# Priorities taken from two backward passes of a kernel's own schedule, and G computed in one step instead of two halves

## The chip, the cores and the metric

The kernel runs on one core of one Trainium2 chip. The metric is device time in microseconds of one execution, the median of three runs. Lower is better.

## The reference

Attention over a packed set of 32 queries, attention of all tokens over that packed result, and then two dense layers with different non-linearities.

```python
# q, k, v: [8, 8, 576, 64], p: [8, 8, 32, 64], all float32
def sm_attn(qq, kk, vv):
    s = scale * np.matmul(qq, kk.transpose(0, 1, 3, 2))
    s = s - np.max(s, axis=-1, keepdims=True)
    a = np.exp(s)
    a = a / (np.sum(a, axis=-1, keepdims=True) + 1e-09)
    return np.matmul(a, vv)
p_packed = sm_attn(p, k, v)
out = sm_attn(q, p_packed, p_packed)
x = out.transpose(0, 2, 1, 3).reshape(4608, 512)
# first dense layer: w_in 512x1024, w_out 1024x512
h = x @ w_in
solu = h * softmax(h)
ln = (solu - mean(solu)) / np.sqrt(var(solu) + 1e-06) * g_ln
x = ln @ w_out
# second dense layer: w_in 512x2048, w_out 2048x512
r = np.maximum(x @ w_in2, 0.0)
return (r * r) @ w_out2
```

The dense weights arrive as 64-bit floats and are decoded to float32 on the chip.

## The kernel before

**Three stages.** Attention and the first dense layer come first; then the first product of the second layer ("z"), then its last product ("o"). All large products split each operand into a rounded part and a remainder (`hi_op`, `lo_op`) and add three products (`mm`, lines 404 to 406). In z and o each 2x2 block product is done with seven products in place of eight, with sums and differences of blocks made on VectorE.

**Stage one** goes over 16 units, a batch entry and a group of four heads each. `pack` loads k and q, turns them (`kT`, `qT`), forms scores `s` with the packed queries (line 560 in the first four units, line 478 later), reduces their maximum `mx` and its negative `nmx` on VectorE, takes the exponential on ScalarE, transposes it (`pt`, line 588), multiplies by v (`ppp`), scales it (`pp`) and transposes that (`ptp`, `ppq`). `unpack` forms the scores of all tokens with `ppq`, normalises them (`a`, `aT`), and multiplies `ppq` by `w_in` into G, 1024 columns in two halves of 512, each in one bank of PSUM (`pg`, line 648). Each half is copied out by ScalarE and then its remainder by VectorE. So attention and `w_in` are folded: `h_tile` gets h of 128 tokens as `aT` times G (`ph`), normalises it and transposes it (`ptv`); `y_stage` multiplies 256 tokens by `w_out` (`py`) and writes to DRAM. For h, the remainders `al` of `aT` are made on VectorE.

**Strips.** z works on six strips of 768 tokens, eight groups of seven products each, and writes its result to DRAM (`g_dram`). o reads it back as `ga`, six strips again, seven products over eight chunks each; `cb` is the split operand. The tiles of `ga` lie in the slots that `y` held in z.

**The planner.** Nothing above runs in program order. Each piece of work is an `Op` with a duration estimate for its engine, an urgency, and its dependencies. `Plan.order` simulates PE, ScalarE, VectorE, GpSimd and one serial DMA server forward in time: of the operations that are ready for a free engine, the one with the lowest urgency goes first. The order in which they start there is the order in which `emit` writes them out, and so the order of the instructions on each engine's queue and of the DMAs on SyncE's queue. Urgencies are written by hand: a formula of the unit or tile number with offsets that stand as constants at the top (`QA`, `GA`, `T0`, `DT`, `WD`, `CS` and so on). A load of n bytes is planned as n/358 ns on the server and lands 2200 ns later:

```python
plan.op(DMA, max(430.0, nbytes / 358.0), at, lambda: queue.dma_start(out=out_(), in_=in_()), r=r, w=w, lag=2200 + spare)
```

**Banks.** Four banks of PSUM (`bank`, a shared ring) serve `s`, `pt`, `ppp`, `ptp`, `pg`, `ptv`, `py` and, later, `pw`, `pz`, `pa`. An operation that needs a bank waits in the plan until `claim` finds one free. `ph` and `px` have banks of their own.

Of the kernel before, what the change touches and what calls it, by code (L numbers as in the profile page):

```python
# [19 lines left out]
PE, ACT, DVE, POOL, DMA = range(5)  # L20
# [70 lines left out]
class Plan:  # L91

    WINDOW = 3413.0

    @staticmethod
# [21 lines left out]
    def either(self, engines, urgency, fn, r=(), w=(), lag=0, claim=(), port=False):  # L120
# [24 lines left out]
        deps.discard(i)  # L145
        self.ops.append(Op(engines, urgency, fn, lag, bufs, deps, port))

    def order(self):
        ops = self.ops
        users = [[] for _ in ops]  # L150
        left = [len(o.deps) for o in ops]
        able = [[] for _ in range(5)]
        busy = [False] * 5
        events = []
        uses = {}
        pe_busy, pe_warm = {}, [False]
        port = 0.0

        def pe_end(t, ns):

            while ns > 1e-6:
                w = int(t / self.WINDOW + 1e-9)
                while len(pe_warm) <= w:
                    share = pe_busy.get(len(pe_warm) - 1, 0.0) / self.WINDOW
                    pe_warm.append(share > 0.74 or (share > 0.5 and pe_warm[-1]))
                slow = 1 if pe_warm[w] else 2
                d = min(ns * slow, (w + 1) * self.WINDOW - t)
                pe_busy[w] = pe_busy.get(w, 0.0) + d
                t += d
                ns -= d / slow  # L170
            return t

        for i, o in enumerate(ops):
            for d in o.deps:
                users[d].append(i)
            for b in o.bufs:
                uses[b] = uses.get(b, 0) + 1
            if not o.deps:
                heapq.heappush(events, (0.0, i, "ready"))
        order = []  # L180

        def claim(i):
            need = [b for b in ops[i].bufs if b.ring and b.ring.shared and b.slot is None]
            for n, b in enumerate(need):
                if len(b.ring.free) <= sum(c.ring is b.ring for c in need[:n]):
                    b.ring.queue.append((ops[i].urgency, i))
                    return False
            for b in need:
                b.slot = b.ring.free.pop(0)
            return True  # L190

        def take(e, t):
            nonlocal port
            while not busy[e] and able[e]:
                _, i = heapq.heappop(able[e])
                o = ops[i]
                if o.engine is not None:
                    continue
                o.engine = e
                busy[e] = True  # L200
                order.append(i)
                if e == POOL or e == DVE and o.port:
                    port = self.span = max(t, port) + o.engines[e]
                else:
                    self.span = pe_end(t, o.engines[e]) if e == PE else t + o.engines[e]
                heapq.heappush(events, (self.span, i, "free"))
                heapq.heappush(events, (self.span + o.lag, i, "done"))

        while events:
            now = events[0][0]  # L210
            while events and events[0][0] <= now:
                t, i, what = heapq.heappop(events)
                o = ops[i]
                if what == "ready":
                    if claim(i):
                        for e in o.engines:
                            heapq.heappush(able[e], (o.urgency, i))
                elif what == "free":
                    busy[o.engine] = False
                else:  # L220
                    for b in o.bufs:
                        uses[b] -= 1
                        if not uses[b] and b.slot is not None:
                            b.ring.free.append(b.slot)
                            for _, j in sorted(b.ring.queue):
                                heapq.heappush(events, (t + 200, j, "ready"))
                            b.ring.queue.clear()
                    for j in users[i]:
                        left[j] -= 1
                        if not left[j]:  # L230
                            heapq.heappush(events, (t + min(self.hop(o.engine, e) for e in ops[j].engines), j, "ready"))
            for e in (PE, ACT, POOL, DVE, DMA):
                take(e, now)
        assert len(order) == len(ops), "the plan is stuck"
        return order

    def emit(self):
        with self.tc.manual_schedule():
            for i in self.order():
                self.ops[i].fn(self.ops[i].engine)  # L240
            for s in reversed(list(self.stacks.values())):
                s.close()
# [3 lines left out]
def kernel(  # L246
# [25 lines left out]
    nc = tc.nc  # L272
# [3 lines left out]
    F1 = moe_w_in.shape[1]  # L276
# [7 lines left out]
    SH = S // 2  # L284
    ST = 256
    AB, GB, RAW, TMP, VR, ET = 4, 4, 1, 2, 1, 1
    QA, GA, HA, TR, UN = 55.91, 149.84, 34.68, -39.93, -11.33
    NK = 4
    WD, WDS, WIS = 99.51, 175.52, 17.0
    GSC = (POOL,)  # L290
    SIN, SOUT = DVE, ACT
    GX = 1
    SUB, KLO, ALO = (POOL,), (DVE,), (DVE,)
    ZSIN, OSIN = DVE, DVE
    SN, FN, LATE = 5.72, -26.79, 3090.0
    YB, ZL, OL, GL0, GL1, GL2, PS, CS = 197.3, 148.71, 20.73, 15.29, 13.31, 32.6, 1.04, 186.23
    NST = NT // ST
    HN = 384
    NSZ = NT // (2 * HN)
# [170 lines left out]
    rows = [min(P, S - j * P) for j in range(KJ)]  # L470

    pbz = [ab.tile([P, 2, HG, 32] if i == 0 else [P, 2, 2, 32], F32, f"pbz{i}") for i in range(3)]
    PAIR = 4 * (0.4336 * SH + 6)

    def pair_mm(ps, lhs, rhs, cs):

# [15 lines left out]
    def pack(at, b, g):  # L492
# [105 lines left out]
        def pp_mm():  # L598
            for j in range(KJ):
                m = rows[j]  # L600
                for e in range(2):
                    nc.tensor.matmul(
                        ppp()[64 * e:64 * e + 64, :2 * D].rearrange("p (h m i) -> p h m i", h=2, m=2),
                        eT()[:m, j, 64 * e:64 * e + 64], vr()[:m, 2 * e:2 * e + 2, j, :].rearrange("p m (h i) -> p h m i", h=2), start=j == 0, stop=j == KJ - 1)
        plan.op(PE, KJ * 267, at + 10, pp_mm, r=[eT, vr], w=[ppp])

        pp = ab.tile([P, 2, P], F32, "pp", tag="s", bufs=2)
        plan.op(DVE, c_dve(256) + 60, at + 12, lambda: nc.vector.scalar_tensor_tensor(
# [18 lines left out]
    def unpack(at, b, g, packed):  # L627
# [10 lines left out]
                out=a()[:, bs, :], in_=s2()[:, :SH].rearrange("p (n t) -> p n t", t=T)), r=[s2], w=[a])  # L638

        gt = m1.tile([P, 1, F1], F32, "G", bufs=GB) if b < GX else m1.tile([P, 2, F1], F32R, "G", bufs=GB)  # L640
        for f in range(F1 // 512):
            pg = bank("pg")
            fs = slice(f * 512, (f + 1) * 512)

            def g_mm(pg=pg, fs=fs):
                for e in range(2):
                    es = slice(64 * e, 64 * e + 64)
                    nc.tensor.matmul(pg()[es, :], ppq()[:, e], wi[2 * g + e]()[:, fs], start=True, stop=True)  # L648
            plan.op(PE, 885, at + GA, g_mm, r=[ppq, wi[2 * g], wi[2 * g + 1]], w=[pg], claim=[gt])
            hi_op(at + GA + 1, 512, lambda fs=fs: gt()[:, 0, fs], pg, [pg], [gt])  # L650
            if b >= GX:
                lo_op(at + GA + 1, 512, lambda fs=fs: gt()[:, 1, fs], pg, lambda fs=fs: gt()[:, 0, fs], [pg, gt], [gt], (DVE,))
# [161 lines left out]
    g_mark = [[[plan.mark("g") for _ in range(4)] for b in range(4)] for st in range(NSZ)]  # L814


    T0, DT = 127.57, 23.948
    PD0, PD = 111.2, 23.139
    UD, UA, U1 = 25.541, 213.28, -45.68
    WI, WO, WOD, YL = 162.35, 266.68, 65.988, 3.36  # L820
    units = [(b, g) for b in range(B) for g in range(NG)]
# [29 lines left out]
    weights_z()  # L851

    ORDER = (1, 2, 6, 5, 7, 3, 4)
    DZ, DO = 5.018, 7.511
    T1 = T0 + DT * NT / P
    TO = T1 + NSZ * 8 * DZ

# [298 lines left out]
            o_products(at, st)  # L1156

    second()
    plan.emit()


# [28 lines left out]
```

## Time and profile before

| | us |
|---|---|
| median of three runs | 1263.37 |
| lowest, highest | 1262.45, 1266.02 |
| the profiled execution | 1262.49 |
| its span, first to last instruction | 1260.4 |
| PE busy in the span | 1205.5 |
| DVE (VectorE) busy | 906.0 |
| ACT (ScalarE) busy | 789.7 |
| POOL (GpSimd) busy | 171.7 |

The profiled execution has 2.1 us outside its span. Times in the trace count from the start of the span. PE's busy time is a union of overlapping matmuls, so the distance between the starts of two matmuls tells more than the duration of one.

### The profile page before, as it was taken

What the parts mean: (1) busy time and instruction counts of PE and PEld (TensorE: products, weight loads), DVE (VectorE), ACT (ScalarE), POOL (GpSimd) and SP (SyncE); (2) the same over time, 40 slices, a digit from 0 to 9 for tenths busy, and PEclk for the clock granted to TensorE, in tenths of its full rate; (3) what the DMA queues carried; (4) which work ended last, traced back from release to release, by engine and by line L of the source; (5) the groups of instructions that cost most, each with busy time, mean ns of one, the idle gap of its engine ahead of it and who ended that gap; (6) DMA issues with size and microseconds to landing.
All of it is one profiled execution on the core that took longest, in us unless ns stands there. A gap on an engine that the chain in (4) does not pass through costs nothing.

```text
span 1260.4 us, 23326 instructions
## 1 busy us (share of the span) xinstructions
PE 1205.5 (96%) x8332; PEld 1101.2 (87%) x8332; DVE 906.0 (72%) x1817; ACT 789.7 (63%) x1678; POOL 171.7 (14%) x181
## 2 busy tenths in 40 slices
PE   4668999999999999999999999999899999999998
PEld 2336788877888789999999999999899999999998
DVE  5888678787766874455686868662678787878786
ACT  2476577666776666577777878777554555555453
POOL 1364323333332340000000000000000000000000
PEclk9878999999999999999999999999899999999999
DMA  8856756776756649465767676753986535343501
GB/s 214 224 154 168 204 156 174 216 197 170 205 150 193 171 125 329 157 200 197 242 199 248 205 249 206 230 166 130 351 341 210 157 121 158 112 151 110 171 32 51
DMA packets 185240, 234.60 MB, mean 186 GB/s; under 512 B 24356, under 2 KB 148772, under 8 KB 184356
## 3 DMA queue, kind: packets, MB, share of 16 engines
q1 hardware_dynamic: 184260, 232.33, 60.2%
q8 instruction: 65, 1.06, 0.4%
q10 hardware_dynamic: 864, 0.79, 0.2%
q14 instruction: 51, 0.42, 0.1%
HBM read 130.55 MB, written 85.98 MB: 172 GB/s over the span
## 4 chain that ended last, share of the span: by engine, by line
PE 78%; DMA 5%; DVE 4%; ACT 3%; issue 1%; SPq 1%; ACTq 0%; DVEq 0%
PE px L404 9%; PE px L406 8%; PE px L405 8%; PE ph L719 7%; PE py L404 5%; PE py L405 5%; PE py L406 5%; PE pa L404 5%; PE pa L406 5%; PE pa L405 5%; PE ptv L762 3%; PE s L478 2%; PE pg L648 2%; PE pz L406 2%; PE pz L405 2%; PE pz L404 2%
## 5 line engine op out<-in xcount | busy, mean ns | idle before, releaser
L386 ACT CAST cb<-ga 128x384 fp32r<-128x384 f32 x336 | 168.0, 513 | 168.3 <-PE px L406 70.9
L389 DVE TENSOR_TENSOR cb<-ga,cb 128x384 fp32r<-128x384 f32 x336 | 180.5, 555 | 60.8 <-ACT cb L386 59.5
L404 PE MATMUL py<-v,wo 128*128 128x256 f32 x576 | 169.3, 294 | 0.0
L405 PE MATMUL py<-v,wo 128*128 128x256 f32 x576 | 163.5, 284 | 0.0
L406 PE MATMUL py<-v,wo 128*128 128x256 f32 x576 | 163.2, 283 | 0.0
L404 PE MATMUL px<-oi,cb 128*128 128x256 f32 x504 | 142.8, 283 | 2.9 <-ACT cb L386 2.9
L406 PE MATMUL px<-oi,cb 128*128 128x256 f32 x504 | 142.5, 283 | 0.8 <-DVE cb L389 0.8
L405 PE MATMUL px<-oi,cb 128*128 128x256 f32 x504 | 142.4, 282 | 0.0
L404 PE MATMUL pa<-oi,cb 128*128 128x256 f32 x504 | 141.4, 281 | 0.0
L406 PE MATMUL pa<-oi,cb 128*128 128x256 f32 x504 | 141.0, 280 | 0.0
L405 PE MATMUL pa<-oi,cb 128*128 128x256 f32 x504 | 141.0, 280 | 0.0
L404 PE MATMUL px<-y,zi 128*128 128x384 f32 x384 | 130.3, 339 | 1.8 <-ACT gw L963 1.7
L405 PE MATMUL px<-y,zi 128*128 128x384 f32 x384 | 129.6, 337 | 0.4 <-DVE y L389 0.3
L406 PE MATMUL px<-y,zi 128*128 128x384 f32 x384 | 129.3, 337 | 0.0
L404 PEld LDWEIGHTS py<-v,wo 128*128 128x128 f32 x576 | 110.6, 192 | 9.1 <-issue 7.8
L967 DVE TENSOR_TENSOR gw<-pz,gw 128x384 f32<-128x384 f32 x96 | 53.2, 554 | 81.1 <-PE pz L406 66.2
L405 PEld LDWEIGHTS py<-v,wo 128*128 128x128 f32 x576 | 110.8, 192 | 0.7
L406 PEld LDWEIGHTS py<-v,wo 128*128 128x128 f32 x576 | 110.6, 192 | 0.0
L907 DVE TENSOR_TENSOR ga<-ga 128x384 f32<-128x384 f32 x192 | 99.7, 552 | 2.6 <-DMA ga<-g_dram 1.9
L404 PEld LDWEIGHTS px<-oi,cb 128*128 128x128 f32 x504 | 96.4, 191 | 3.2 <-ACT cb L386 3.2
L406 PEld LDWEIGHTS px<-oi,cb 128*128 128x128 f32 x504 | 96.5, 191 | 1.1 <-DVE cb L389 1.1
L975 ACT ACTIVATE gw<-gw 128x384 f32<-128x384 f32 x115 | 60.2, 523 | 57.5 <-DVE gw L967 57.1
(180 smaller groups left out, 2990.8 us busy)
## 6 DMA issues: line engine op xcount, KB each, us to landing
g_dram<-gw SPq DMA_DIRECT2D x192, 192.0 KB
ga<-g_dram SPq DMA_DIRECT2D x96, 384.0 KB
zi<-z_dram SPq DMA_DIRECT2D x28, 512.0 KB
oi<-o_dram SPq DMA_DIRECT2D x24, 512.0 KB
kr<-in_k_dram SPq DMA_DIRECT2D x16, 576.0 KB
qr<-in_q_dram SPq DMA_DIRECT2D x16, 576.0 KB
q<-qT SPq DMA_DIRECT2D x64, 144.0 KB
y_dram<-ysb SPq DMA_DIRECT2D x72, 128.0 KB
```

The costliest lines, as they stand in the source:

```text
L386: plan.op(ACT, c_act(cols, sbuf=r[0].pool not in (psm, psh, pso)), at, lambda: nc.scalar.copy(out_(), in_()), r=r, w=w)
L389: plan.either(on(cols, *engines), at, lambda e: vec[e].tensor_tensor(out_(), in_(), hi_().bitcast(F32), op=ALU.subtract), r=r, w=w, port=i ...
L404: nc.tensor.matmul(ps, lh, rh, start=first, stop=False, skip_group_check=onto)
L405: nc.tensor.matmul(ps, lh, rl, start=False, stop=False, skip_group_check=onto)
L406: nc.tensor.matmul(ps, ll, rh, start=False, stop=last, skip_group_check=onto)
L478: nc.tensor.matmul(ps()[64 * e:64 * e + 64, :SH], cols(lhs, e), cols(rhs, e)[:, cs], start=True, stop=True)
L648: nc.tensor.matmul(pg()[es, :], ppq()[:, e], wi[2 * g + e]()[:, fs], start=True, stop=True)
L719: nc.tensor.matmul(ph()[:, fs], al[l]()[:, g], g_tiles[b, g]()[:, r, fs], start=ends[0] and g == 0 and t == 0, stop=ends[1] and g == NG - ...
L762: nc.tensor.transpose(pt()[:, c * P:(c + 1) * P], e()[:, (4 * t + c) * P:(4 * t + c + 1) * P], ident)
L907: plan.op(DVE, c_dve(cols), at, lambda: nc.vector.tensor_tensor(out_(), in0(), in1(), op=op), r=r, w=w, port=True)
L967: plan.op(DVE, c_dve(HN), when(p, SN), lambda: nc.vector.tensor_tensor(t(), ps()[:, :HN], t(), op=ALU.add), r=[t, ps], w=[t])
L975: nc.scalar.activation(t(), t(), AF.Relu)
```

## The change

After the first forward plan, `backward` plans the same work from the end to the start, on the engines and in the PSUM slots that the forward plan chose, taking first what ended last. The distance of each operation from the end of that plan becomes its urgency, in place of the hand-written one, and `order` runs forward again. This is done twice (`PASSES = 2`). The hand-written urgencies so only start the first plan; some of their constants are changed. The two halves of G become one operation of PE that claims two banks. `al` moves from VectorE to GpSimd (`ALO`). Three durations in the plan become longer (`PAIR`, `pp_mm`, G).

```diff
+    def reset(self):
+        for o in self.ops:
+            o.engine = None
+            for b in o.bufs:
+                b.slot = None
+                if b.ring:
+                    b.ring.free, b.ring.queue = list(range(b.ring.bufs)), []
+
+    def backward(self):
+
+        ops, ends = self.ops, self.ends
+        deps = [set(o.deps) for o in ops]
+        slots = {}
+        for b in dict.fromkeys(b for o in ops for b in o.bufs if b.slot is not None):
+            slots.setdefault((b.ring, b.slot), []).append(b)
+        for bufs in slots.values():
+            bufs.sort(key=lambda b: ends[b.touched[0]])
+            for a, b in zip(bufs, bufs[1:]):
+                deps[b.touched[0]].update(a.touched)
+        left = [0] * len(ops)
+        for i, d in enumerate(deps):
+            d.discard(i)
+            for j in d:
+                left[j] += 1
+        able = [[] for _ in range(5)]
+        busy = [False] * 5
+        free, starts = [0.0] * len(ops), [0.0] * len(ops)
+        port = 0.0
+        events = [(0.0, i, "ready") for i in range(len(ops)) if not left[i]]
+        heapq.heapify(events)
+        while events:
+            now = events[0][0]
+            while events and events[0][0] <= now:
+                t, i, what = heapq.heappop(events)
+                e = ops[i].engine
+                if what == "ready":
+                    heapq.heappush(able[e], (-ends[i], i))
+                    continue
+                busy[e] = False
+                for j in sorted(deps[i]):
+                    left[j] -= 1
+                    free[j] = max(free[j], t + self.hop(ops[j].engine, e) + ops[j].lag)
+                    if not left[j]:
+                        heapq.heappush(events, (free[j], j, "ready"))
+            for e in (PE, ACT, POOL, DVE, DMA):
+                if not busy[e] and able[e]:
+                    _, i = heapq.heappop(able[e])
+                    busy[e] = True
+                    starts[i] = now + ops[i].engines[e]
+                    if e == POOL or e == DVE and ops[i].port:
+                        port = starts[i] = max(now, port) + ops[i].engines[e]
+                    heapq.heappush(events, (starts[i], i, "free"))
+        end = max(starts)
+        for o, t in zip(ops, starts):
+            o.urgency = round((end - t) / 1e3, 6)
+
     def order(self):
         ops = self.ops
+        self.reset()
+        self.ends = [0.0] * len(ops)
...
+                self.ends[i] = self.span
...
-    def emit(self):
+    def emit(self, passes):
+        order = self.order()
+        for _ in range(passes):
+            self.backward()
+            order = self.order()
         with self.tc.manual_schedule():
-            for i in self.order():
+            for i in order:
                 self.ops[i].fn(self.ops[i].engine)
...
-    QA, GA, HA, TR, UN = 55.91, 149.84, 34.68, -39.93, -11.33
+    QA, GA, HA, TR, UN = 15.37, 149.84, 34.68, -39.93, -15.5
...
-    WD, WDS, WIS = 99.51, 175.52, 17.0
+    WD, WDS, WIS = 101.7, 187.465, 17.0
...
-    SUB, KLO, ALO = (POOL,), (DVE,), (DVE,)
+    PASSES = 2
+    SUB, KLO, ALO = (POOL,), (DVE,), (POOL,)
...
-    YB, ZL, OL, GL0, GL1, GL2, PS, CS = 197.3, 148.71, 20.73, 15.29, 13.31, 32.6, 1.04, 186.23
+    YB, ZL, OL, GL0, GL1, GL2, PS, CS = 189.17, 148.71, 20.73, 15.29, 13.31, 32.6, 1.04, 186.23
...
-    PAIR = 4 * (0.4336 * SH + 6)
+    PAIR = 4 * (0.4336 * SH + 6) + 85
...
-        plan.op(PE, KJ * 267, at + 10, pp_mm, r=[eT, vr], w=[ppp])
+        plan.op(PE, KJ * 280 + 60, at + 10, pp_mm, r=[eT, vr], w=[ppp])
...
-        for f in range(F1 // 512):
-            pg = bank("pg")
-            fs = slice(f * 512, (f + 1) * 512)
-
-            def g_mm(pg=pg, fs=fs):
+        pgs = [bank("pg") for _ in range(F1 // 512)]
+
+        def g_mm():
+            for f in range(F1 // 512):
                 for e in range(2):
                     es = slice(64 * e, 64 * e + 64)
-                    nc.tensor.matmul(pg()[es, :], ppq()[:, e], wi[2 * g + e]()[:, fs], start=True, stop=True)
-            plan.op(PE, 885, at + GA, g_mm, r=[ppq, wi[2 * g], wi[2 * g + 1]], w=[pg], claim=[gt])
+                    nc.tensor.matmul(pgs[f]()[es, :], ppq()[:, e], wi[2 * g + e]()[:, f * 512:(f + 1) * 512], start=True, stop=True)
+        plan.op(PE, 1870, at + GA, g_mm, r=[ppq, wi[2 * g], wi[2 * g + 1]], w=pgs, claim=[gt])
+        for f, pg in enumerate(pgs):
+            fs = slice(f * 512, (f + 1) * 512)
...
-    T0, DT = 127.57, 23.948
-    PD0, PD = 111.2, 23.139
+    T0, DT = 119.52, 22.152
+    PD0, PD = 133.89, 25.885
...
-    DZ, DO = 5.018, 7.511
+    DZ, DO = 4.851, 7.511
```

## Rows read from the trace of the kernel before

**Rows 1.** The page: PE's busy share in 40 slices, in tenths.
```profile
PE   4668999999999999999999999999899999999998
```

**Rows 2.** Busy time of each engine by stage (columns named in the first row).
```profile
core 0: us, PE busy (x) PEld busy (x) DVE busy (x) ACT busy (x) POOL busy (x), PEclk, DMA share, GB/s
0.00:118.80 118.80, 74.22 (x340) 43.46 (x341) 93.00 (x157) 60.58 (x114) 47.11 (x49) 0.87 0.73 189
118.80:530.60 411.80, 410.95 (x2931) 341.63 (x2930) 292.50 (x597) 269.72 (x592) 124.60 (x132) 1.00 0.65 188
530.60:893.60 363.00, 360.70 (x2051) 356.96 (x2049) 227.68 (x449) 276.06 (x584) 0.00 (x0) 1.00 0.65 210
893.60:1260.40 366.80, 359.68 (x3015) 359.19 (x3015) 292.80 (x617) 183.36 (x391) 0.00 (x0) 0.99 0.49 160
```

**Rows 3.** PE's waits in 0 to 120 us: total us, times, longest.
```profile
PE pt L588 <- ACT e L575: 16.0, 6, 7.0
PE s L560 <- DVE kT L537: 7.3, 1, 7.3
PE ptp L618 <- DVE pp L608: 5.7, 3, 3.9
```

**Rows 4.** DVE in order of time, 77 to 92 us: start, duration, what.
```profile
77.93 1.21 DVE L725 TENSOR_REDUCE nm<-ph 128x1 f32<-128x1024 f32 x1
...
82.60 0.45 DVE L564 TENSOR_REDUCE mx<-s 128x1 f32<-128x288 f32 x1
82.97 1.36 DVE L548 STREAM_TRANSPOSE qT<-qr 128x1152 f32<-128x1152 f32 x1
84.26 0.41 DVE L564 TENSOR_REDUCE mx<-s 128x1 f32<-128x288 f32 x1
...
86.39 0.20 DVE L570 TENSOR_SCALAR nmx<-mx 128x1 f32<-128x1 f32 x1
```

**Rows 5.** PE in order of time, 75 to 92 us.
```profile
76.29 2.21 PE L560 MATMUL s<-kT,pbz 128*128 128x288 f32 x8
78.33 3.60 PE L696 MATMUL ph<-G,aT 128*128 128x512 f32 x8
88.98 0.69 PE L588 MATMUL pt<-ident,e 128*128 128x128 f32 x2 [7.05 <-ACT e L575]
```

**Rows 6.** DVE in order of time, 20 to 27 us.
```profile
24.86 0.74 DVE L422 TENSOR_SCALAR wi<-wi 128x1024 int32<-128x1024 int32 x1 [2.34 <-ACT wi L419]
...
26.14 0.43 DVE L608 SCALAR_TENSOR_TENSOR pp<-ppp,rs,mask 128x256 f32<-128x256 f32 x1
```

**Rows 7.** PE in order of time, where stage o begins.
```profile
896.42 0.46 PE L404 MATMUL px<-oi,cb 128*128 128x256 f32 x1 [2.87 <-ACT cb L386]
```

**Rows 8.** The chain that ended last, 870 to 925 us: start, us, what.
```profile
890.91 5.84 DMA ga<-g_dram
...
898.44 0.21 PE px L404
...
903.35 0.20 PE px L406
...
904.02 0.12 PE px L405
```

**Rows 9.** The same chain, two pieces of G's matmuls.
```profile
395.32 1.01 PE pg L648 x4
...
461.00 1.87 PE pg L648 x8
```

**Rows 10.** Groups of instructions on DVE and POOL: count, busy us, mean ns.
```profile
L389 DVE TENSOR_TENSOR al<-aT,ah 128x128 fp32r<-128x128 f32 x56 | 19.0, 349 | 3.0 <-ACT ah L386 2.9
L801 POOL TENSOR_TENSOR wx<-wx 128x128 f32<-128x128 f32 x29 | 13.5, 467 | 2.6 <-DVE wx L801 0.5
```

**Rows 11.** Instructions on tile `al`: ns min/median/max.
```profile
L389 DVE TENSOR_TENSOR al<-aT,ah x70: 209/282/2090, 94.3 to 496.6; 128x128 fp32r<-128x128 f32 x56, 128x64 fp32r<-128x64 f32 x14
```

**Rows 12.** Instructions on tile `pg`: ns min/median/max.
```profile
L386 ACT CAST G<-pg x28: 568/585/592, 69.1 to 464.5; 128x512 fp32r<-128x512 f32 x28
L389 DVE TENSOR_TENSOR G<-pg,G x28: 624/682/693, 69.7 to 465.1; 128x512 fp32r<-128x512 f32 x28
```

More of the change, by code (lines that the diff above doesn't have):

```diff
@@ L1158 @@
     second()
-    plan.emit()
+    plan.emit(PASSES)
 _INS = ['q', 'k', 'v', 'p', 'moe_w_in', 'moe_w_out', 'moe_g_ln', 'moe2_w_in', 'moe2_w_out']
```

## The prediction

> **What bounds the kernel now.** I read first the page's slices of PE's busy share [rows 1]: after the first four of 40 slices PE stands at 8 or 9 tenths to the end. So there is one engine to argue about, and one stretch where it is not full. Then the busy time by stage [rows 2]. In the first 118.8 us PE is busy for 74.2 us, and its clock is granted at 0.87 of full speed. From 118.8 to 530.6 us it lacks 0.9 us, in stage z 2.3 us, in stage o with the tail 7.1 us. Idle time of PE, 55 us in all, is thus for four fifths (44.6 us) a matter of the ramp. In the ramp VectorE is busy 93.0 of 118.8 us, so it is nearly as much the limit as any chain is. In the next stretch it has 411.8 - 292.5 = 119 us to spare.
>
> Third, PE's waits in the ramp [rows 3]. The first 7.3 us wait for the first loads and their transposes, and no order removes them. 16.0 us are waits of the transposes `pt` for the exponential, 5.7 us of `ptp` for `pp`. The reader is to see that both end a short VectorE step (`nmx`, `pp`) that long VectorE steps of other work can stand in front of. Two places show it. In the fourth unit the scores are done at 76.29 + 2.21 = 78.5 us [rows 5]; the two `mx` and `nmx`, 0.45 + 0.41 + 0.20 = 1.06 us of work, run at 82.60, 84.26 and 86.39, with a 1.36 us transpose and reductions of h of 1.21 us in front and between [rows 4]. PE runs dry at 78.33 + 3.60 = 81.93 us and waits 7.05 us [rows 5]. Taken back to back they would end near 79.6, not at 86.6. In the first unit `pp` sits at 26.14 behind a decode of w_in that itself kept VectorE idle for 2.34 us waiting for ScalarE [rows 6]: from 22.52 (24.86 - 2.34) to 26.14 are 3.6 us.
>
> Fourth, the change from z to o. PE waits 2.87 us for the first `cb` [rows 7], which hangs on a 5.84 us load of `ga`, and then its matmuls come 0.21 us apart until 903.35, where 0.12 follows [rows 8]: half the clock, and of 903.35 - 898.44 = 4.9 us the share 1 - 0.12/0.21 = 0.43 is lost, 2.1 us. The change costs 2.87 + 2.1 = 5.0 us.
>
> **The change part by part.**
>
> *Urgencies from the backward plan.* No instruction is added or removed; order is all that changes. The distance from the end is what the four cases above lack: `mx`, `nmx` and `pp` head long chains (exponential, transposes, two more products, scores of all tokens, h) and get the earliest due time, while decodes and reductions with slack go behind. The two places are worth 7.0 + 3.6 = 10.6 us if all of it reaches PE; moving 1.06 us in front of other work delays that by about 1 us. It does not all reach PE, since VectorE is 93.0 of 118.8 us full [rows 2] and what is pushed back is needed for the next h. The bounds are 0 (PE starves somewhere else for the same time) and 16.0 + 5.7 = 21.7 us (all such waits go) [rows 3]. I take 6 us, a little over half of the two places that I can name. At the change to o the plan sees a load that frees late: products of the last z group that read the slots of `ga` can be taken earlier, by up to the four groups that `px` has banks for. Bounds 0 and 5.0 us; I take half, 2.5 us, since the plan prices a `ga` load of 393,216 bytes at 1.1 + 2.2 = 3.3 us where [rows 8] has 5.84. In the full stretch PE has 0.9 us of idle to give [rows 2], so there an order can gain nothing but less switching between kinds of matmul: 0, with some 4 us either way (20 switches at about the 0.15 to 0.2 us worked out next).
>
> *G in one operation.* The trace has both forms. A half alone takes 1.01 us, two halves in a row 1.87 [rows 9]: 2 x 1.01 - 1.87 = 0.15 us a unit, and one return to the other kind of matmul less. Of the 12 units after the ramp I count one whose halves lie together, so 11 x 0.15 = 1.7 us, with the returns about 2 us. Bounds 0 (backward urgencies would have put them together anyway) and 16 x 0.2 = 3.2. I take 2. The price is two banks of four held at once. While the second is drained, ScalarE needs 585 ns and VectorE 682 ns for it [rows 12]; another user of a bank can wait that much longer, 1.27 us a unit. I price it at nothing: `ph` has its own banks and is there to be run. Without that cover it is 16 x 1.27 = 20 us.
>
> *`al` to GpSimd.* VectorE gives up 70 steps; at the 349 ns mean of the 56 wide ones [rows 10] that is 24.4 us. GpSimd gets 70 steps for which the nearest row is a subtraction of the same shape, 467 ns [rows 10], 32.7 us more on an engine with 411.8 - 124.6 us free [rows 2]. h waits for `al` 0.1 to 0.2 us longer, behind h tiles planned ahead. I take 0: VectorE isn't the limit where `al` runs (94.3 to 496.6 us [rows 11]), and the two that lie in the ramp free under 2 us.
>
> The trace shows that the two engines get in each other's way: the same `al` takes 209 ns at best and 2090 at worst [rows 11]. The Trainium skill, SBUF — State Buffer, section "Who interferes with whom", says that a VectorE instruction with two SBUF inputs and a GpSimd instruction that reads SBUF use one shared port, and that the one that comes second is blocked for the other's whole instruction. That speaks against the move: with every new GpSimd step blocking VectorE for its whole length the sum would be about 8 us smaller, and by the median `al` of 282 ns [rows 11], close to the best, it stays as it is.
>
> *Constants and longer plan durations* only move the start of the plan or its estimates towards what the trace shows (1870 ns for G is the row); 0.
>
> Sum: 6 + 2.5 + 2 = 10.5 us off the profiled execution's 1262.49 (span 1260.4 and 2.1 around it), so 1252.0. The median of the runs stands 0.9 us above that execution: 1252.9, say 1253.
>
> **The rivals.** A measurement of this kernel can tell some 0.3%, 3.8 us, from no change: below 1259.6 is faster, above 1267.2 slower.
>
> Nothing reaches the chip. The plan gets shorter, but the chip's order-bound waits only change places: the ramp stays at VectorE's 93 us of work plus the load latency, and 2 us of G remain or are lost to switching. Time about 1261 to 1264. For it: `pp` waited behind a decode whose delay came from ScalarE, which the plan must foresee to avoid. Against: the 7.05 us of [rows 5] are mere priority among ready work. Chance 0.13.
>
> The shared port eats it. The new GpSimd steps block VectorE for all of their 32.7 us, 8.3 more than it gave up, and that reaches PE through a stretch in which PE has no slack: 1253 + 8 = 1261, about no change. The section of the Trainium skill named above, on SBUF — State Buffer, is what would make it so. Against: 119 us of idle VectorE. Chance 0.04.
>
> Loads come late. In the place of hand-set leads for `ga` (13.31 to 32.6, `GL0` to `GL2`), due times now come from a plan that gives such a load 3.3 us, where one took 5.84. At six places (the change to o and five changes of strip) a load due at the last moment would come 2.5 us late; with the slow matmuls that followed the one wait in [rows 7, 8], 2.5 + 2.1. So 6 x 2.5 = 15 to 6 x 4.6 = 28 us, and the 2.5 us at the change are not gained: 1270 to 1283. It decides only if the loads are issued at their due time; the plan issues them when slot and server are free, and the DMA share in o is 0.49 [rows 2]. Chance 0.14.
>
> The two banks stall PE: 20 us as above, 1273. It decides where the units' G falls among `py` and `ptv` with no `ph` ready. PE's 410.95 of 411.8 us [rows 2] leave no place to hide it, yet the plan can choose the moment. Chance 0.09.
>
> More comes out of the ramp. If most of the 21.7 us go, and the whole 5.0 us and the 2 us of G with them, the gain is 18 to 29 us: 1235 to 1246. VectorE's load in the ramp (93.0 of 118.8) speaks against most of it. Chance 0.12 for all below 1246.
>
> **How the numbers follow.** My own case, 1246 to 1259, has the remaining 0.48. Faster is 0.48 + 0.12 = 0.60, same 0.13 + 0.04 = 0.17, slower 0.14 + 0.09 = 0.23. For 8 in 10 the range leaves out about 0.08 at the low end (below 1238) and 0.12 at the high one (above 1276): 1238 to 1276. The likeliest case alone is 1246 to 1259.
>
> **What would show it.** In the profile after: the stretch until PE is full is some 6 us shorter; the total of `pt` waiting for the exponential falls from 16.0 to about 10; after the fourth unit's scores `mx`, `mx`, `nmx` stand together; G's matmuls stand in pieces of eight at about 1.87 us; the first matmul of o waits under 1.5 us. From the end of the ramp to o's start the distance stays within 4 us of 411.8 + 363.0. Wrong it would be if PE showed new waits of a microsecond or more in o (loads), or idle time between 120 and 530 us (banks, port), or if the ramp's waits for `pt` merely became waits for `aT` or `ph`.

## The result and the profile after

The changed kernel takes 1275.15 us (median of five runs, 1272.44 to 1277.79). The kernel before, run beside it on the same chip, takes 1265.47 (1262.45 to 1267.47). The ratio is 1.0073, with a 95% interval of 1.0055 to 1.0091: 0.7% slower, where 1253 was forecast and 1276 was the upper end of the range. The profiled execution took 1277.79, with a span of 1276.0. Lines of the changed file are numbered about 65 higher than those of [rows 1 to 12].

The page of the changed kernel: PE's slices, and the shares of the chain that ended last.

```profile
PE   3668999999999999999999999999999999999998
...
PE 68%; DMA 10%; DVE 8%; ACT 6%; issue 3%; SPq 2%; POOL 2%; ACTq 0%; DVEq 0%; POOLq 0%
```

The slices look as before [rows 1]: a tenth is too coarse to show the loss. The chain does show a change of kind: loads are 10% of it, where the page of the kernel before has 5%:

```profile
PE 78%; DMA 5%; DVE 4%; ACT 3%; issue 1%; SPq 1%; ACTq 0%; DVEq 0%
```

The busy time by stage says where. Columns as in [rows 2]; z begins at 553.10 and o at 913.30.

```profile
0.00:118.80 118.80, 73.27 (x305) 37.17 (x305) 84.57 (x152) 57.16 (x110) 51.54 (x51) 0.83 0.73 185
118.80:553.10 434.30, 418.88 (x2976) 347.86 (x2977) 282.63 (x537) 270.25 (x599) 151.24 (x199) 1.00 0.63 181
553.10:913.30 360.20, 357.55 (x2031) 354.59 (x2030) 230.06 (x454) 267.25 (x565) 0.00 (x0) 1.00 0.66 210
913.30:1276.00 362.70, 358.13 (x3025) 357.67 (x3023) 291.09 (x616) 181.46 (x391) 0.00 (x0) 1.00 0.49 161
```

Stage one ends 22.5 us later (553.1 against 530.6). From there to the end the kernel is 6.9 us shorter: 1276.0 - 553.1 = 722.9 against 1260.4 - 530.6 = 729.8. Of these 6.9 us 1.4 are no gain: 12 of the `py` matmuls, 0.12 us each, that the kernel before runs after z has begun now run ahead of it. So the loss lies in stage one alone, and it has two parts. After 118.8 us PE now stands idle for 434.3 - 418.9 = 15.4 us, where [rows 2] have 0.9. Before 118.8 us the idle time is much as it was (45.5 against 44.6), but PE got 305 matmuls done there instead of 340, at a clock of 0.83 instead of 0.87. The 45 more matmuls after it (what the ramp left undone, and the 12 `py`), at 418.88 / 2976 = 0.14 us each, make up most of the 7 us by which PE is busy longer in all of stage one (73.27 + 418.88 = 492.15, against 74.22 + 410.95 = 485.17).

PE's waits in 0 to 120 us (total us, times, longest), which answer to [rows 3]:

```profile
PE s L625 <- DVE kT L602: 14.4, 3, 10.4
PE pt L653 <- ACT e L640: 7.2, 2, 4.0
PE ptp L683 <- DVE pp L673: 5.5, 3, 2.9
PE s L543 <- ACT ppq L451: 5.1, 2, 2.8
```

The waits for the exponential fell from 16.0 to 7.2. That was forecast as the work of the urgencies, but the urgencies alone don't do it. The same line in two kernels told of below, first the kernel before with the passes and nothing else, then the changed kernel with G split again:

```profile
PE pt L653 <- ACT e L640: 14.9, 5, 8.1
PE pt L653 <- ACT e L640: 16.0, 4, 6.9
```

In the changed kernel scores now wait 14.4 us for `kT` instead of 7.3, and 5.1 us for `ppq`. The chain that ended last names the loads behind it (start, us, what):

```profile
2.33 7.20 DMA kr<-in_k_dram
9.56 1.30 DVE kT L602 x2
...
17.55 6.69 DMA wraw<-in_moe_w_in_dram
...
30.73 7.45 DMA wraw<-in_moe_w_in_dram
38.20 8.93 DMA wraw<-in_moe_w_in_dram
```

The first load of k is now issued behind a load of `vr`. It lands 7.2 us after its issue, when the plan counts 589,824 / 358 + 2200 ns = 3.85 us. In the kernel before it was issued ahead of `vr`, and landed about 4.6 us after its issue. The first scores start 3.1 us later for it (10.41 us, against 7.31). This late start doesn't account for the loss, though. The changed kernel with G split again starts its scores at 7.03 us and takes 1278; planned with a landing of 2800 ns it starts them at 10.90 and takes 1264:

```profile
7.03 4.18 PE L625 MATMUL s<-kT,pbz 128*128 128x288 f32 x8 [7.03 <-DVE kT L602]
10.90 3.59 PE L625 MATMUL s<-kT,pbz 128*128 128x288 f32 x8 [10.90 <-DVE pbz L582]
```

From 120 to 545 us no wait stands out; the largest three of eleven kinds:

```profile
PE ptp L683 <- DVE pp L673: 3.3, 3, 1.6
PE pt L653 <- ACT ysb L851: 2.2, 2, 1.8
PE s L543 <- DVE v L454: 2.0, 2, 1.1
```

PE runs dry briefly in many places, behind whichever product happens to come next.

The fourth unit, DVE from 74 to 84 us, to be laid beside [rows 4]:

```profile
74.20 0.43 DVE L629 TENSOR_REDUCE mx<-s 128x1 f32<-128x288 f32 x1
...
76.75 1.38 DVE L613 STREAM_TRANSPOSE qT<-qr 128x1152 f32<-128x1152 f32 x1 [1.46 <-DMA pr<-in_p_dram]
78.05 0.42 DVE L629 TENSOR_REDUCE mx<-s 128x1 f32<-128x288 f32 x1
78.39 1.21 DVE L500 SCALAR_TENSOR_TENSOR wraw<-wraw 128x1024 f32<-128x1024 uint32 x1
79.52 0.20 DVE L635 TENSOR_SCALAR nmx<-mx 128x1 f32<-128x1 f32 x1
```

Other work still stands between the three, and a wait of VectorE for a load (1.46 us). Yet PE's wait for the exponential behind them fell from 7.05 us [rows 5] to 4.02.

The start of o, PE in order of time, which answers to [rows 7]:

```profile
913.09 0.33 PE L471 MATMUL px<-y,zi 128*128 128x384 f32 x1
913.26 0.28 PE L469 MATMUL px<-oi,cb 128*128 128x256 f32 x1
913.38 0.28 PE L470 MATMUL px<-oi,cb 128*128 128x256 f32 x1
...
920.13 0.39 PE L471 MATMUL px<-oi,cb 128*128 128x256 f32 x1 [1.08 <-DVE cb L454]
```

The 2.87 us wait is gone, and with it the stretch at half clock of [rows 8]: the matmuls come 0.12 us apart at once. One wait of 1.08 us follows, the only one that PE's waits show from 913 us to the end.

Last, G. ScalarE's copy that completes `ppq` for the fifth unit, and PE's matmuls that use it:

```profile
119.60 0.27 ACT L451 COPY ppq<-ptp 128x128 f32<-128x128 f32 x1
...
165.00 1.94 PE L712 MATMUL pg<-wi,ppq 128*64 128x512 f32 x8
```

G is one piece of eight, as the change says. But it starts 45 us after its operand is there. I call this G's delay: from the end of the copy of `ppq` to the unit's first `pg` matmul, as the mean of the twelve units after the fourth. It is 8.6 us before and 28 us after.

### The profile page after: what moved, and what is told of

It is laid out like the page before. It is cut to its first block, busy times and chain, and to the rows that moved or that the text cites. A ratio compares the mean times of both kernels' runs of the same rounds, so it can differ in the third digit from the quotient of the medians.

```text
span 1276.0 us, 23354 instructions
## 1 busy us (share of the span) xinstructions
PE 1207.8 (95%) x8332; PEld 1097.3 (86%) x8332; DVE 888.3 (70%) x1756; ACT 776.1 (61%) x1664; POOL 202.8 (16%) x249
## 4 chain that ended last, share of the span: by engine, by line
PE 68%; DMA 10%; DVE 8%; ACT 6%; issue 3%; SPq 2%; POOL 2%; ACTq 0%; DVEq 0%; POOLq 0%
PE px L469 8%; PE px L471 8%; PE px L470 8%; PE pa L469 5%; PE pa L471 5%; PE pa L470 5%; PE ph L785 4%; PE py L469 4%; PE py L470 4%; PE py L471 4%; SPq L438 2%; PE pz L469 2%; PE pz L471 2%; PE pz L470 2%; DMA wraw<-in_moe_w_in_dram 2%
## 5 line engine op out<-in xcount | busy, mean ns | idle before, releaser
L471 PEld LDWEIGHTS pa<-oi,cb 128*128 128x128 f32 x504 | 95.2, 189 | 0.1
```

Source lines behind the costliest of these rows:

```text
L471: nc.tensor.matmul(ps, ll, rh, start=False, stop=last, skip_group_check=onto)
```

## The experiments

Three theories stood against each other. **Two banks:** `claim` gives G both banks or none, so operations that want one bank overtake it; G, then h, then PE come late. **The port:** the `al` on GpSimd slow VectorE down. **The landing:** the plan lets loads land sooner than they do, and an order drawn close to the plan pays for that on the chip. Beside these stood the plainest explanation: each edit draws a different order of all operations, and the time scatters with it. The expectations number them: theory 1 is that the backward urgencies of themselves put PE's feeders too close to their use, 2 the port, 3 the two banks, 4 the constants or durations, 5 the scatter, 6 the landing. The kernels below leave out no part of the computation. Every time is a median, and every ratio is to the kernel before on the same chip, whose medians lie between 1264.55 and 1266.22; a difference between kernels that ran on different chips is uncertain by as much.

**The changed kernel without the passes.**

```diff
-    PASSES = 2
+    PASSES = 0
```

> The changed kernel with PASSES = 0: its constants, its merged G, its al on GpSimd and its durations stay, only the hand-written urgencies order the work. Theory 1 (the backward urgencies put PE's feeders so close to their use that small lateness on the chip becomes waits in 120 to 440 us) expects the waits of PE in that stretch, 16 us in the changed kernel, to fall under 5 us and the time to 1262 to 1268. Theory 2 (al on GpSimd takes the shared port) and theory 3 (G holds two of four banks) expect those waits to stay, since both parts stay: 1275 or more.

Measured: 1297.48, ratio 1.0253 (1.0235 to 1.0272). So inside the changed kernel the passes gain 22 us, and its other parts without them cost 31. Theory 1 expected 1262 to 1268 and is refuted. z begins at 568.4.

**The kernel before with the two passes and nothing else.** `reset`, `backward` and `emit(passes)` are added; the old constants and durations, G in two halves and `al` on VectorE stay.

> The kernel before with the two backward passes alone: its constants, G in two halves, al on VectorE, its durations. Theory 1 expects what the changed kernel shows: some 10 to 16 us of new PE waits after the ramp, 1272 to 1282. Theories 2 and 3 expect no such waits, as neither part is there: 1255 to 1266, with some gain in the ramp.

Measured: 1259.28, 0.9949 (0.9936 to 0.9963): faster by 0.5%, where theory 1 expected 1272 to 1282. Its windows:

```profile
0.00:118.80 118.80, 74.65 (x357) 43.14 (x357) 91.10 (x152) 61.43 (x116) 51.03 (x48) 0.86 0.74 190
118.80:531.00 412.20, 410.00 (x2912) 338.04 (x2912) 296.35 (x605) 267.33 (x589) 121.50 (x130) 1.00 0.65 188
```

Stage one ends as it did before (531.0), and the gain lies behind it: 1257.1 - 531.0 = 726.1 against 729.8. The urgencies alone win the change to o and win nothing in the ramp. The first holds for nearly every kernel of this document: from z's start to the end 16 of the 17 with passes take 720 to 726 us (the one planned with 1600 ns, below, 734), and the three without 728 to 731.

**One more part on top of the passes.** Each of these four is the kernel just shown with one part of the change added.

G in one operation (the diff of G in the change, and nothing else):

> The kernel before with the two passes and G in one operation of two banks; al, constants and the other durations as before. The passes alone gained 7 us. If the two banks are what turned that into a loss (theory 3), 1270 or more, with new PE waits where G or its neighbours come late. If the loss lies in the new constants or durations (theory 4), 1256 to 1261, 2 us less for G's switches.

Measured: 1275.4, 1.0094 (1.0075 to 1.0112), 16.1 us over the passes alone. G's delay is 29.1 us where the passes alone have 7.7, and PE lacks 21.1 us after the ramp:

```profile
118.80:551.40 432.60, 411.54 (x2899) 343.83 (x2898) 293.38 (x589) 263.51 (x582) 125.69 (x132) 0.98 0.60 173
```

`al` on GpSimd:

```diff
-    SUB, KLO, ALO = (POOL,), (DVE,), (DVE,)
+    SUB, KLO, ALO = (POOL,), (DVE,), (POOL,)
```

> The kernel before with the two passes and al on GpSimd. If the shared port matters (theory 2), 1267 or more and PE waits after 120 us on VectorE's results. Otherwise 1256 to 1262.

Measured: 1269.79, 1.0036 (1.0018 to 1.0054), 10.5 us over the passes alone. That is in the range of theory 2, but the other VectorE steps of stage one, 686 in each of the two traces, take 402.7 us in sum here and 404.0 in the passes alone, so `al` on GpSimd didn't lengthen them.

The new constants (`QA`, `UN`, `WD`, `WDS`, `YB`, `T0`, `DT`, `PD0`, `PD`, `DZ`):

> The kernel before with the two passes and the new constants (QA, UN, WD, WDS, YB, T0, DT, PD0, PD, DZ); G in halves, al on VectorE, old durations. If the constants start the passes from a worse plan (theory 4), 1270 or more. If they are only a start that the passes replace, as the prediction has it, 1257 to 1262.

Measured: 1266.54, 1.001 (0.9995 to 1.0024), 7.3 us over the passes alone. The ten runs spread from 1260.95 to 1271.28.

The longer plan durations:

```diff
-    PAIR = 4 * (0.4336 * SH + 6)
+    PAIR = 4 * (0.4336 * SH + 6) + 85
...
-        plan.op(PE, KJ * 267, at + 10, pp_mm, r=[eT, vr], w=[ppp])
+        plan.op(PE, KJ * 280 + 60, at + 10, pp_mm, r=[eT, vr], w=[ppp])
```

> The kernel before with the two passes and the longer durations of the pair products and of pp in the plan; nothing else. The durations are nearer to the trace, so if they only make the plan truer, 1255 to 1260. If they are part of the loss, 1265 or more.

Measured: 1275.16, 1.0083 (1.0068 to 1.0098), 15.9 us over the passes alone. No instruction became longer, only the plan's estimate of two. Each of the four parts costs something on top of the passes. Singly they cost 16, 10, 7 and 16 us, and all together also 16. So these prices don't add.

**How far the order alone moves the time.** Two kernels change only the number of passes: four in the changed kernel, and three on the passes alone.

```diff
-    PASSES = 2
+    PASSES = 4
```

> The changed kernel with four backward passes instead of two; all its parts stay, only the order differs. If the loss belongs to the parts (bank, port, constants, durations), 1272 to 1280. If it is the luck of one order among many nearly equal ones (theory 5), it lands anywhere between 1262 and 1285, and 8 us or more from the changed kernel would show it.

Measured: 1269.57, 1.0037 (1.0020 to 1.0054), 5.6 us less than the changed kernel.

```diff
-    PASSES = 2
+    PASSES = 3
```

> The kernel before with three backward passes and nothing else. If the passes themselves are worth some 6 us, 1255 to 1262, as with two. If two passes were a lucky draw (theory 5), 1265 or more.

Measured: 1261.48, 0.9979 (0.9968 to 0.9991), 2.2 us more than with two. The new constants and the longer plan durations above change no instruction either, only the order, and moved the time by 7.3 and 15.9 us. So a difference of up to some 16 us between two kernels with different orders can't be put down to the part that differs by that pair alone.

**`al` taken back.** First by the plan (`ALO = (DVE,)` in the changed kernel, everything ordered anew):

> The changed kernel with al back on VectorE, passes and merged G kept. Theory 2 expects the waits after 120 us to go and 1262 or less. Theories 1 and 3 expect 1272 to 1280, about the changed kernel's time.

Measured: 1285.19, 1.0163 (1.0138 to 1.0188), 10 us worse than the changed kernel. Then with the changed kernel's whole order kept: the plan still puts `al` on GpSimd, and only its instructions are issued on VectorE, in the place that the order gives them.

```diff
-    def lo_op(at, cols, out_, in_, hi_, r, w, engines=(POOL,)):
-        plan.either(on(cols, *engines), at, lambda e: vec[e].tensor_tensor(
+    def lo_op(at, cols, out_, in_, hi_, r, w, engines=(POOL,), run=None):
+        plan.either(on(cols, *engines), at, lambda e: vec[run or e].tensor_tensor(
...
-                    split(at + HA, cs.stop - cs.start, a_tiles[b, g], *al, ALO, vs=view, vo=to)
+                    split(at + HA, cs.stop - cs.start, a_tiles[b, g], *al, ALO, vs=view, vo=to, run=DVE)
```

> The changed kernel with its whole order kept, as planned with al on GpSimd, but with the 70 al steps issued on VectorE in the place where the plan starts them. Theory 2 (blocking on the shared port, and al late on GpSimd) expects 1265 or less. If al's engine is no part of the loss, 1273 to 1280.

Measured: 1281.11, 1.0131 (1.0110 to 1.0151), 6 us worse than the changed kernel. This is the one run that removes the GpSimd steps without drawing a new order, and it takes longer. On the passes alone the move cost 10.5 us, here taking it back costs 6 to 10, where theory 2 expected 1265 or less: no constant price. The port itself does show in the kernel before. Its longest `al` on VectorE lies beside a GpSimd step of the same length:

```profile
220.60 2.09 DVE L389 TENSOR_TENSOR al<-aT,ah 128x64 fp32r<-128x64 f32 x1
220.50 2.10 POOL L389 TENSOR_TENSOR wx<-wx,wh 128x896 fp32r<-128x896 f32 x1 [0.40 <-ACT wh L386]
```

Ten of the 70 take 444 to 2090 ns there, each with a GpSimd step beside it; of the 39 without one none takes more than 289. But the loss isn't that: the other 688 VectorE steps of stage one take 403.0 us in sum in the changed kernel, and 402.3 with `al` issued on VectorE. In the changed kernel the instruction is as dear as was estimated from [rows 10] (467 ns); the instructions on tile `al` there, ns min/median/max:

```profile
L454 POOL TENSOR_TENSOR al<-aT,ah x70: 317/458/1299, 102.5 to 513.0; 128x128 fp32r<-128x128 f32 x56, 128x64 fp32r<-128x64 f32 x14
```

**G split again in the changed kernel.**

```diff
-        plan.op(PE, 1870, at + GA, g_mm, r=[ppq, wi[2 * g], wi[2 * g + 1]], w=pgs, claim=[gt])
+            plan.op(PE, 885, at + GA, g_mm, r=[ppq, wi[2 * g], wi[2 * g + 1]], w=[pg], claim=[gt])
```

The last line stands in the loop over the two halves again, with one bank for each.

> The changed kernel with G in two operations of one bank each, passes and al on GpSimd kept. Theory 3 expects the waits after 120 us to go and 1262 or less, though G itself costs 2 us more. Theories 1 and 2 expect 1272 to 1280.

Measured: 1278.45, 1.0098 (1.0081 to 1.0114), 3.3 us more than the changed kernel. G's delay is back at 7.5 us, and yet PE still lacks 13.8 us after the ramp:

```profile
118.80:548.00 429.20, 415.39 (x2955) 347.08 (x2954) 274.88 (x528) 271.00 (x595) 152.53 (x199) 1.00 0.62 178
```

That is a blow to the two banks as the whole answer: here the delay of G is cured and the time isn't. Something else keeps PE waiting as well.

**G in one operation in the kernel before**, with no passes and hand-written urgencies:

> The kernel before, no passes, with G in one operation of two banks (planned at 1870 ns). My prediction's term has 2 us less. If an operation that needs two banks at once is passed over while neighbours take single ones (theory 3), G comes late and 1280 or more follows, with waits of PE that fall on G's users.

Measured: 1308.37, 1.0348 (1.0309 to 1.0388): 43 us slower. G's delay is 51.6 us. The longest, ScalarE's copy and PE's matmuls of the tenth unit:

```profile
244.48 0.26 ACT L386 COPY ppq<-ptp 128x128 f32<-128x128 f32 x1
...
350.39 1.94 PE L647 MATMUL pg<-wi,ppq 128*64 128x512 f32 x8
```

106 us pass between them. PE lacks 28.2 us after the ramp (454.8 - 426.59), and here even its clock drops to 0.95 over that stretch:

```profile
118.80:573.60 454.80, 426.59 (x2935) 352.00 (x2932) 297.05 (x595) 267.85 (x588) 117.12 (x128) 0.95 0.58 169
```

Two banks at once are a real price, then, when nothing makes up for it. That they delay G holds in every kernel here: 19.8 to 51.6 us in the ten with G in one operation, 4.6 to 9.4 in the ten with two halves. The waits of PE that were expected to fall on G's users don't show, however. PE's longest waits after the ramp, here and in the kernel of passes and one G:

```profile
PE s L478 <- DMA k<-kT: 10.0, 4, 6.5
PE ptv L828 <- ACT e L816: 4.5, 3, 2.2
```

So the delay of G is shown, and the way from it to PE's idle time isn't.

**The landing.** One number of the plan is changed in the changed kernel, 2200 ns to 2800, 2700 and 1600; no instruction changes, only the order drawn with it.

```diff
-        ... r=r, w=w, lag=2200 + spare)
+        ... r=r, w=w, lag=2800 + spare)
```

> The changed kernel with every load planned to land 2800 ns after the server is done with it, not 2200. Theory 6: the loads on the chip land later than the plan has them, ScalarE and VectorE stand before a load with ready work queued behind, and the tight plan has no slack for it; then the time falls to 1260 to 1270 and PE's waits after 120 us to under 8 us. If lateness of loads is not it, 1272 or more.

Measured: 1264.37, 0.9993 (0.9981 to 1.0005).

> The changed kernel with every load planned to land after 1600 ns instead of 2200, further from the 2.6 to 6.3 us that loads in its chain took from issue to use. Theory 6 (loads later than planned) expects more waits on loads and 1280 or more. A mere redraw of the order (theory 5) expects anything from 1262 to 1285.

Measured: 1297.41, 1.0255 (1.0222 to 1.0287).

> The changed kernel with 2700 ns, next to the 2800 that gave 1264. Theory 6 expects 1262 to 1269. Theory 5 expects anything from 1262 to 1285, so 1272 or more speaks for it.

Measured: 1265.14, 1.0000 (0.9985 to 1.0015). So 1600, 2200, 2700 and 2800 ns give 1297, 1275, 1265 and 1264 us: longer landings in the plan make for a shorter time on the chip, step by step. The step from 2200 to 2700 is 10 us, less than the 15.9 us by which an order drawn again has moved the time; the one from 1600 to 2200 is 22. G's delay falls along with it (34.8, 28.3, 19.8 and 21.6 us), so these four kernels don't hold the two causes apart. Stage one with 2700 and with 1600 ns:

```profile
0.00:118.80 118.80, 78.80 (x326) 41.04 (x327) 88.26 (x152) 59.27 (x113) 50.46 (x52) 0.90 0.73 185
118.80:538.20 419.40, 413.08 (x2956) 343.25 (x2955) 280.90 (x537) 269.15 (x592) 152.13 (x195) 1.00 0.64 186
```

```profile
0.00:118.80 118.80, 77.16 (x308) 39.19 (x309) 87.12 (x152) 55.11 (x110) 40.22 (x45) 0.83 0.82 200
118.80:562.10 443.30, 423.35 (x2964) 351.82 (x2963) 282.33 (x535) 271.12 (x596) 160.66 (x203) 0.98 0.59 172
```

PE's idle time after the ramp is 6.3 us with 2700 ns, 15.4 with 2200 and 20.0 with 1600. The direct sign was to be ScalarE's decodes of `w2raw` waiting for their load. From 118 to 530 us such waits are 12.9 us with 1600, 11.1 with 2200, 2.6 with 2700 and 1.9 with 2800; that much fits.

On the passes alone, with 2600 ns in place of 2200 (the same edit):

> The kernel before with two passes and a planned landing of 2600 ns. Theory 6 with the passes' own gain expects 1252 to 1260, at or below the 1259 of the passes alone. If truer loads give nothing of themselves, 1260 to 1270.

Measured: 1262.9, 0.9983 (0.9966 to 0.9999): 3.6 us more than with 2200, within what an order drawn again gives. A longer landing isn't a gain in itself.

**Both together.** G split and a landing of 2700 ns in the changed kernel:

> The changed kernel with loads planned to land after 2700 ns and G in two operations of one bank each. If the two banks still cost under truer loads (theory 3), 1260 or less, faster than the kernel before and 5 us or more below the merged G at 2700 ns (1265). If banks cost only through the tight plan, 1263 to 1268.

Measured: **1253.59, 0.9906 (0.9885 to 0.9927)**, faster than both kernels.

```profile
0.00:118.80 118.80, 82.04 (x383) 44.96 (x383) 93.96 (x162) 62.45 (x122) 49.28 (x52) 0.91 0.81 204
118.80:529.40 410.60, 406.04 (x2902) 339.51 (x2899) 279.23 (x535) 268.97 (x590) 151.57 (x194) 1.00 0.61 174
529.40:890.50 361.10, 358.18 (x2030) 354.56 (x2029) 226.04 (x445) 269.81 (x568) 0.00 (x0) 1.00 0.68 223
890.50:1253.10 362.60, 358.51 (x3026) 357.77 (x3024) 292.11 (x617) 181.33 (x391) 0.00 (x0) 1.00 0.49 161
```

The first 118.8 us hold 383 matmuls instead of 305, at a clock of 0.91; after them PE lacks 4.6 us; G's delay is 4.6 us. The time is 5.7 us under that of the passes alone (1259.28), no more than an order drawn again moves. z begins at 529.4, and the end keeps its gain (723.7 from there). But ScalarE's waits for `w2raw` are 7.6 us here, exactly what they are in the split kernel with 2200 ns, which is 25 us slower. The passes alone have 10.3 and are among the fastest. So these waits don't follow the time, and that late loads of them are the mechanism isn't shown.

The same with `al` back on VectorE:

> The same with al back on VectorE. If al on GpSimd costs (theory 2), 3 us or more below the run with it on GpSimd. If it doesn't, within 3 us of it or above.

Measured: 1262.29, 0.9971 (0.9959 to 0.9983), 8.7 us more. The part of the change that was suspected of the port is no loss in this order.

| G, landing in the plan | 2200 ns | 2700 ns |
|---|---|---|
| two banks at once | 1275.15 | 1265.14 |
| two halves | 1278.45 | 1253.59 |

The table is the answer as far as the runs give one, and each of its cells is one drawn order. The later landing is worth 10 us with two banks and 24.9 with two halves. Splitting is worth 11.6 us with the later landing and -3.3 with the earlier one, where PE stands idle 13.8 us even without the two banks.

## Why the prediction was wrong

**The step that failed** is the one that held the full stretch to "0, with some 4 us either way", since an order had nothing to gain there but less switching, and beside it the 0 for constants and longer plan durations. PE's 0.9 us of idle time there was read as a bound on what could be gained. It bounds no loss: a full engine can only become idle, and the prediction gave the stretch no loss beyond those 4 us except through its rivals. The stretch and the ramp before it cost 22.5 us, of which 14.5 are new idle time of PE after the ramp. On top of the passes alone, constants cost 7.3 us, durations 15.9 and `al` 10.5, three items of the sum that stood at zero.

**Ramp, -6.** The sign was seen in the changed kernel (waits for the exponential 16.0 to 7.2, where 10 was forecast), but not its cause: with the urgencies alone these waits are 14.9. And the gain wasn't there: PE waited for `kT` and `ppq` in their place. That is the bound of 0, by which PE starves somewhere else, and with fewer matmuls done in the ramp it was worse than that. "No order removes" the first 7.3 us was nearly right, but an order can lengthen them: the first scores start between 7.0 and 10.9 us in these kernels, without the time following.

**Change to o, -2.5.** Right, and too small: from z's start to the end 5.5 us came off (6.9 less the 1.4 of `py`), in the passes alone 3.7.

**G, -2, and its two banks at nothing.** The pieces are of eight as forecast, but they save less. From the first matmul of a piece to the start of what follows, a half takes 0.96 us in the kernel before, and eight take 1.81 in the changed kernel and 1.91 with the passes and one G: 0.01 to 0.11 us a unit, where 0.15 was read from durations. The price of the banks was wrong. It was taken from how long a neighbour waits for a bank, 1.27 us a unit; what it costs is that G itself waits for two to be free together, 28 us a unit against 8.6. The cover, "`ph` has its own banks", would fail when the G that `ph` reads is what comes late; PE's waits don't show that, so this is argued. Measured, it is +16.1 us on the passes, +43 in the kernel before, +11.6 with the later landing, and -3.3 in the changed kernel as it stands. The rival of the two banks had the sign and nearly the time (1273), and a chance of 0.09. That the time agrees is in part luck: with G split again the changed kernel is no faster.

**Loads late.** This rival (chance 0.14) put the loss into the changes of strip in o, and there PE waits 1.1 us in all. The landing in the plan does move the time, but in stage one.

**`al`, 0.** 458 ns is the estimated 467. The sign of the move depends on the order around it. The Trainium skill, SBUF — State Buffer, section "Who interferes with whom", lets a GpSimd step block VectorE on their shared port. The trace of the kernel before agrees, with the `al` of 2090 ns shown above. But in the one comparison that keeps the order, issuing `al` on VectorE takes 6 us more, so that rule isn't what made the changed kernel slow.

**What stays open.** Why a longer landing helps the changed order and not that of the passes alone. How much of each part's price is a property of the part, and how much is the luck of one drawn order: the pairs that change only the number of passes move by 2.2 and 5.6 us, those that change only the plan's constants or durations by 7.3 and 15.9, so the prices of single parts are uncertain in size. Of the four of G only the 43 us in the kernel before stand clear of that. How a late G makes PE idle isn't shown. Which late event begins each of the short idle times after the ramp isn't settled.

## What to carry to other kernels

Where an order is drawn by a planner, a full engine isn't a floor under the loss: any edit of an estimate, an engine or a bank redraws everything, so change one part at a time and draw a few orders of each before giving it a price. Here edits of the plan's numbers alone moved the time by up to 16 us. An operation that takes two slots of a shared pool at once pays with its own delay behind those that want one, so look at how long its operand lies ready, not at how long its neighbours wait. Before judging better priorities, check the plan's landing times of loads against the trace; here 500 ns more in the plan and G in two halves turned +0.7% into -0.9%, though a longer landing gained nothing on the passes alone.

## What was unexpected of the hardware

At the start, where many loads are issued one behind the other, some land later than the 5.84 us of [rows 8]: 7.2 us from issue for the first k, and 6.7 to 8.9 us on the chain for three loads of `wraw`. With a load of `vr` issued ahead of that of k, the first step that reads k started 7.2 us after k's issue, and 6.8 in the other kernel with that order. In the 18 kernels that issue k ahead of `vr` it was 4.2 to 6.1 us, so part of the step from 4.6 to 7.2 is the spread that loads show without it.

A VectorE subtraction of 128x64 that takes some 0.2 us took 2.09 us beside a GpSimd step of 2.10 us.
